# A spectral layer with one table loaded by another queue, two DMAs swapped, and its last steps in another order

## Chip, core and metric

The kernel runs on one core of a Trainium2 chip. The metric is the device time of one execution in microseconds; the time before is the median of nine runs. A profile is of one execution.

## What is computed

Two kinds of layer alternate twice. A is a filter in the frequency domain over the whole 2048 x 1024 input, B is a dense block with the Mish activation; each follows a layer norm and is added to its input.

```python
def _A_ref(x, w_r, w_i):
    X = rfft2(x.astype(float32), axes=(-2, -1))
    X = X * (w_r + 1j * w_i)
    return irfft2(X, s=(S, D), axes=(-2, -1)).astype(bfloat16)

def _B_ref(x, w1, b1, w2):
    h = einsum("bsd,df->bsf", x, w1) + b1
    act = h * tanh(softplus(h))
    return einsum("bsf,fd->bsd", act, w2)

x = x + _A_ref(_layernorm(x), A_w_r, A_w_i)
x = x + _B_ref(_layernorm(x), B_w1, B_b1, B_w2)
x = x + _A_ref(_layernorm(x), A_w_r, A_w_i)
x = x + _B_ref(_layernorm(x), B_w1, B_b1, B_w2)
```

S is 2048, D is 1024, the inner width of B is 3584; inputs and output are bf16.

## The kernel before

The program order of each engine is written out by hand: a helper adds an instruction to an engine's list and works out which semaphores it has to wait for, from the last writers and readers of each buffer. An engine works through its list strictly in order, so an instruction that waits holds up everything listed behind it. This holds for the issuing queues too: SP (SyncE), ACT (ScalarE) and POOL (GpSimd) issue DMAs one after the other, and a DMA that waits for a semaphore holds up the next. All DMAs are issued at L251, so the tiles tell them apart.

Both transforms are products with tables of sines and cosines. A spectral layer (`layer_A`, L711) goes through these stages:

- `s1` (L620): a first short transform along the tokens, for the whole input, into the buffer Y.
- Then eight groups, 0 to 7, each of two of the sixteen remainders of the token frequency. A group goes through four kinds of step, each in two halves (0 and 1). A step is named by three digits: kind, group, half.
  - **2** (`s2`, L733, matmuls L741): the transform along the model dimension, into Z. Half 0 is copied out of PSUM by ACT (L776), half 1 by ACT for groups 0 to 2 and by DVE from group 3 on (L778). In layer 0 a group's filter is put into its layout beside this step (`filter_bins`, matmuls L1002, copies on DVE L1013 and on ACT L1017), beside half 1 for groups 0 and 1 and half 0 for the others.
  - **3** (`s3`, L780, matmuls L786 to L789): the transform along the rest of the tokens with the group's **forward table** (FT). ACT copies the result out (L793), and DVE multiplies it by the filter in four operations (L797, L799, L802, L804), into YK.
  - **4** (`i1`, L807, L815): the inverse of 3 with the group's backward table (BT), copied by ACT (L826) into V; for group 7 half by DVE, half by ACT (L578, L574).
  - **5** (`i2`, L828, L840 and L872): the inverse along the model dimension with the matrix BD, into U: the group's components. ACT copies (L884), DVE for halves 531 and 551 (L882), both for group 7.
- `u_turn` (L886): when half 1 of kind 5 is copied out, the group's components are stored to DRAM (`u_scratch`), and one that was stored before is read back in another layout (`u_back`, L908) into UT. For groups 0 to 6 both are issued by SP: first the store of group g, then the read-back of g - 1. Group 7 is stored by ACT in two halves, and its read-backs are the last ones (`u_last`, L914), by SP and ACT.
- After a few matmuls that keep PE busy (L652, L657), the last short transform (`i4`, L1035, matmuls L1041) reads UT and so waits for all the read-backs. It belongs to the dense layer's start.

Every step takes one of four pairs of PSUM banks in turn, so a step also waits until the step four before it has been copied out; in layer 0 a filter step takes a pair too.

The forward tables sit in a ring of three buffers, as the backward ones do. `open_tables` (L664) loads the first ones: tables 0 and 1, in layer 1 also forward table 2. In layer 0 SP issues these, in layer 1 POOL. The later ones are loaded by POOL in the loop over the steps: the forward table of group g + 2 after step 3, half 1 of group g (L952 to L954). In layer 0 so is forward table 2, after step 301. POOL has other loads in layer 0: the filter rows of groups 2 to 7 (`load_wr`, L984), each as a real and an imaginary part, and the store of the finished filter for layer 1 (`keep_filter`, L1020). SP's list in layer 0 goes on after the tables with small constants, BD among them.

The order of the steps, the same in both layers, is a list of numbers (`order_A`, L976): PE, ACT and DVE all get their instructions in it.

Of the kernel before, what the change touches and what calls it, by code (L numbers as in the profile page):

```python
# [180 lines left out]
class KB:  # L181
# [482 lines left out]
    def open_tables(self, li):  # L664

        self.li = li
        self.WT = self.ring("WT", 4 if li else 8, 2048, [2, 512])
        self.FTr = self.ring("FT", 3, 1536, [2, 384])
        self.BTr = self.ring("BT", 3, 1536, [2, 384])
        if li == 0:  # L670
            self.WR = self.ring("WR", 3, 4096, [2, 2, 512])
        for g in range(2):
            self.load_w(g)
        for g in range(2 + li):
            self.load_tabs(g, li == 0)
        for g in range(2):
            self.load_btabs(g, li == 0)

    def rest_of_filter(self):

        self.WT += [self.alloc(f"WT{i}", self.o["WT"] + 2048 * i, [2, 512]) for i in range(4, 8)]
        gate = Res("gate")
        for r in self.r_xr[1:3]:
            gate.inherit(r)
        for g in (2, 3):
            self.load_w(g, [gate])

    def load_tabs(self, g, sp=False):
        b = self.FTr[g % 3]
        self.dma(self.sp if sp else self.pool, b.ap, self.con["FT"][g], f"ft{g % 3}{sp}", writes=[b.res])  # L690

    def load_btabs(self, g, sp=False):
        b = self.BTr[g % 3]
        self.dma(self.sp if sp else self.pool, b.ap, self.con["BT"][g], f"bt{g % 3}{sp}", writes=[b.res])
# [9 lines left out]
    def load_w(self, g, after=()):  # L704
        if self.li == 0:
            self.load_wr(self.wr(g), g)
            return
        i = 2 * g % 8
        self.dma(self.pool, self.wt_pair(i), self.w_d[g], f"wt{g % 4}", reads=[self.r_wd[g]] + list(after), writes=[w.res for w in self.WT[i:i + 2]])

    def layer_A(self, li):  # L711
# [13 lines left out]
        def filter_bins(g):  # L725
            ps, banks, _ = self.pair()
            self.filter_bins(g, ps, banks, self.wr(g), WT[2 * g % 8:2 * g % 8 + 2], o["WT"] + 2048 * (2 * g % 8),
                             self.JT, self.r_jt, dve)
# [51 lines left out]
        def s3(g, i):  # L780

            ps, banks, _ = self.pair()
            z, ft = zslot(g, i), FT[g % 3]
            t = ft.ap[:, i, :]
            fns = [
                lambda e: e.matmul(ps[:, 0:512], t[:, 0:128], z.ap[:, 0, :], start=True, stop=False),  # L786
                lambda e: e.matmul(ps[:, 512:1024], t[:, 0:128], z.ap[:, 1, :], start=True, stop=False),
                lambda e: e.matmul(ps[:, 512:1024], t[:, 128:256], z.ap[:, 0, :], start=False, stop=True),
                lambda e: e.matmul(ps[:, 0:512], t[:, 256:384], z.ap[:, 1, :], start=False, stop=True),  # L789
            ]  # L790
            self.group(fns, reads=[z.res, ft.res], writes=banks)
            x = X[(2 * g + i) % 4]
            self.op(act, lambda e: e.activation(x.ap.rearrange("p a b -> p (a b)"), ps, ACT.Copy, scale=SIG),  # L793
                    reads=banks, writes=[x.res])
            wt, yk = WT[(2 * g + i) % 8], YK[(2 * g + i) % 6]
            ta, tb = T[2 * i], T[2 * i + 1]
            self.op(dve, lambda e: e.tensor_tensor(ta.ap, x.ap, wt.ap[:, 0:1, :].to_broadcast([P, 2, 512]), ALU.mult),  # L797
                    reads=[x.res, wt.res], writes=[ta.res])
            self.op(dve, lambda e: e.tensor_tensor(tb.ap, x.ap, wt.ap[:, 1:2, :].to_broadcast([P, 2, 512]), ALU.mult),  # L799
                    reads=[x.res, wt.res], writes=[tb.res])  # L800
            yk.res.begin()
            self.op(dve, lambda e: e.tensor_tensor(yk.ap[:, 0, :], ta.ap[:, 0, :], tb.ap[:, 1, :], ALU.subtract),  # L802
                    reads=[ta.res, tb.res], parts=[yk.res])
            self.op(dve, lambda e: e.tensor_tensor(yk.ap[:, 1, :], tb.ap[:, 0, :], ta.ap[:, 1, :], ALU.add),  # L804
                    reads=[ta.res, tb.res], parts=[yk.res])

        def i1(g, i):  # L807

            ps, banks, _ = self.pair()
            yk, bt, v = YK[(2 * g + i) % 6], BT[g % 3], V[g % 2]  # L810
            t = bt.ap[:, i, :]
            fns = []
            for c in range(4):
                for part in range(2):
                    fns.append(lambda e, c=c, part=part: e.matmul(  # L815
                        ps[:, c * 256:(c + 1) * 256], yk.ap[:, part, c * P:(c + 1) * P], t[:, (128, 0)[part]:(384, 256)[part]],
                        start=(part == 0), stop=(part == 1)))
            self.group(fns, reads=[yk.res, bt.res], writes=banks)
            if i == 0:
                v.res.begin()  # L820
            src = ps.rearrange("p (c n) -> p c n", n=P)
            if g == 7:
                for b, prog in enumerate((dve, act)):
                    self.copy(prog, v.ap[:, 4 * b:4 * b + 4, i, :], src[:, 4 * b:4 * b + 4, :], [banks[b]], [], parts=[v.res])
                return
            self.op(act, lambda e: e.activation(v.ap[:, :, i, :], src, ACT.Copy), reads=banks, parts=[v.res])  # L826
# [59 lines left out]
        def u_turn(g, half):  # L886

            u = U[g % 3]
            if g == 7:
                h = slice(8 * half, 8 * half + 8)  # L890
                if half == 0:
                    u_back(6)
                self.dma(act, self.u_d[g][:, h, :], u.ap[:, h, :], f"uwh{half}", reads=[u.res], writes=[self.r_ud7[half]])
                if half:
                    u_last()
            elif half:
                self.dma(sp, self.u_d[g], u.ap, f"uw{g % 3}", reads=[u.res], writes=[self.r_ud[g]])
                if g:
                    u_back(g - 1)

        def open_ut():
# [6 lines left out]
        def u_back(g):  # L908
            if self.UT is None:
                open_ut()  # L910
            self.dma(sp, self.UT.ap[g:P:8, :, :], self.u_d[g].rearrange("l r n -> r l n"), f"usp{g % 3}",
                     reads=[self.r_ud[g]], parts=self.r_ut)

        def u_last():  # L914

            def back(prog, half, q, n):
                l = slice(32 * q, 32 * q + 32 * n)
                self.dma(prog, self.UT.ap[7 + 64 * half:P if half else 64:8, l, :], self.u_d[7][l, 8 * half:8 * half + 8, :].rearrange("l r n -> r l n"),
                         f"ul{half}{q}", reads=[self.r_ud7[half]], parts=self.r_ut[q:q + n])
            back(sp, 0, 0, 2)  # L920
            back(sp, 0, 2, 2)
            for q in range(4):
                back((act, sp)[q % 2], 1, q, 1)
# [17 lines left out]
        for stage, g, h in self.order_A():  # L941
            if stage == 2:
                s2(g, h)
                if li == 0 and h == (g < 2):
                    filter_bins(g)
                    if g in (0, 1):
                        load_w(g + 5)
                    elif g == 4:
                        load_w(7)
            elif stage == 3:  # L950
                s3(g, h)
                if h:  # L952
                    if li <= g < 6:
                        load_tabs(g + 2)  # L954
                    if li == 0:
                        self.keep_filter(g)
                    elif g < 4:
                        load_w(g + 4)
            elif stage == 4:
                i1(g, h)  # L960
                if h and g < 6:
                    load_btabs(g + 2)
            else:
                i2(g, h)
                u_turn(g, h)
# [9 lines left out]
    @staticmethod  # L975
    def order_A():  # L976


        order = ("200 201 210 300 211 301 220 310 400 221 311 401 230 320 410 500 231 321 411 501 330 331 420 510 240 511 421 241 "
                 "250 251 340 341 520 350 430 260 521 431 440 261 351 441 530 531 360 361 450 451 540 541 550 270 551 271 460 461 "  # L980
                 "370 371 560 561 470 471 570 571")
        return [tuple(map(int, w)) for w in order.split()]

    def load_wr(self, wr, g):  # L984
# [798 lines left out]
```

## Time and profile before

| what | value |
|---|---|
| median of 9 runs | 931.34 us (930.1 to 934.52) |
| profiled execution | 934.52 us |
| its span in the profile | 932.7 us |
| PE (matmul) busy | 881.4 us, 94% of the span |
| DVE, ACT, POOL busy | 66%, 47%, 17% |
| first layer A, steps of kinds 2 to 5 | from 37.2 us to the last store at 106.99 us |
| second layer A, the same | from 496.97 us to the last store at 558.33 us |
| share of PE in the chain that ended last | 83% |
| share of DMAs in that chain | 6% |

How to read it: the span is measured inside the core, from the first to the last instruction; the execution's time is a little longer. A row of the timeline gives start, length, engine, line of the kernel, operation and tiles; in brackets is how long the engine stood idle ahead of it, and what ended that idle time. PEld is the load of a matmul's stationary operand and runs beside PE. The chain that ended last is followed back from the last instruction, at each step to what released it. The granted clock is PE's, as a share of full speed.

### The profile page before, as it was taken

What the parts mean: (1) busy time and instruction counts of PE and PEld (TensorE: products, weight loads), DVE (VectorE), ACT (ScalarE), POOL (GpSimd) and SP (SyncE); (2) the same over time, 40 slices, a digit from 0 to 9 for tenths busy, and PEclk for the clock granted to TensorE, in tenths of its full rate; (3) what the DMA queues carried; (4) which work ended last, traced back from release to release, by engine and by line L of the source; (5) the groups of instructions that cost most, each with busy time, mean ns of one, the idle gap of its engine ahead of it and who ended that gap; (6) DMA issues with size and microseconds to landing.
All of it is one profiled execution on the core that took longest, in us unless ns stands there. A gap on an engine that the chain in (4) does not pass through costs nothing.

```text
span 932.7 us, 13616 instructions
## 1 busy us (share of the span) xinstructions
PE 881.4 (94%) x5503; PEld 471.8 (51%) x5503; DVE 619.7 (66%) x985; ACT 436.0 (47%) x645; POOL 159.9 (17%) x187
## 2 busy tenths in 40 slices
PE   0889889999999999999999988999999999999998
PEld 0667476444444444444446766764444444444443
DVE  7788367687689667558866765666747665554473
ACT  7989385456213385520019965847650015552000
POOL 5633003970003652010121200000000000000000
PEclk9999999999999999999999998999999999999999
DMA  9969861684877488364732894444156545732432
GB/s 290 284 203 292 211 182 52 236 283 102 294 243 231 151 306 314 130 211 153 271 108 98 233 220 133 159 154 163 58 189 192 176 150 194 277 119 82 172 123 109
DMA packets 145839, 175.99 MB, mean 189 GB/s; under 512 B 66904, under 2 KB 124344, under 8 KB 145656
## 3 DMA queue, kind: packets, MB, share of 16 engines
q1 hardware_dynamic: 132816, 128.29, 44.4%
q0 software_dynamic: 10864, 45.19, 13.5%
q10 hardware_dynamic: 2096, 1.64, 0.6%
q8 instruction: 43, 0.70, 0.3%
q14 instruction: 20, 0.16, 0.1%
HBM read 130.78 MB, written 40.89 MB: 184 GB/s over the span
## 4 chain that ended last, share of the span: by engine, by line
PE 83%; DMA 6%; DVE 4%; ACT 3%; SPq 2%; POOL 1%; issue 1%; ACTq 0%; DVEq 0%; POOLq 0%
PE PS L1329 33%; PE PS L1230 29%; PE PS L1190 6%; PE PS L815 3%; PE PS L741 3%; DMA ARENA<-in_B_w_dram 2%; PE PS L840 2%; SPq L251 2%; PE PS L1041 2%; POOL ARENA L1123 1%; DMA ARENA<-in_A_x_dram 1%; PE PS L1151 1%; DMA ARENA<-u_scratch 1%; DMA u_scratch<-ARENA 1%; PE PS L786 1%
## 5 line engine op out<-in xcount | busy, mean ns | idle before, releaser
L1329 PE MATMUL PS<-ARENA 128*128 128x512 bf16 x1568 | 340.4, 379 | 0.7 <-DMA ARENA<-in_B_w_dram 0.7
L1230 PE MATMUL PS<-ARENA 128*128 128x512 bf16 (+1 forms) x1288 | 280.5, 379 | 0.8 <-DVE ARENA L1235 0.8
L1329 PEld LDWEIGHTS PS<-ARENA 128*128 128x128 bf16 x1568 | 153.2, 98 | 185.6 <-DVE ARENA L1372 1.0
L1235 DVE TENSOR_TENSOR ARENA<-PS,ARENA 128x512 f32<-128x512 f32 x230 | 157.1, 691 | 101.1 <-PE PS L1230 93.2
L1230 PEld LDWEIGHTS PS<-ARENA 128*128 128x128 bf16 x1288 | 125.3, 98 | 153.5 <-DVE ARENA L1235 3.5
L1240 ACT ACTIVATE ARENA<-ARENA,B 128x512 bf16<-128x512 f32 x138 | 98.8, 721 | 69.3 <-DVE ARENA L1235 64.0
L574 ACT ACTIVATE ARENA<-PS 128x512 f32<-128x512 f32 (+3 forms) x86 | 61.6, 727 | 114.4 <-PE PS L1230 93.1
L1123 POOL TENSOR_TENSOR ARENA<-ARENA 128x512 bf16<-128x512 bf16 x56 | 71.8, 1282 | 74.5 <-DVE ARENA L523 60.4
L452 ACT ACTIVATE ARENA<-XS 128x1024 bf16<-128x1024 bf16 x60 | 63.2, 1053 | 36.3 <-DVE XS L1380 33.0
L1190 PE MATMUL PS<-ARENA 128*128 128x256 bf16 (+1 forms) x528 | 75.1, 300 | 3.2 <-DVE ARENA L1156 1.7
L1354 DVE TENSOR_TENSOR ARENA<-ARENA 128x3584 bf16<-128x3584 bf16 x32 | 63.9, 2017 | 0.0
L1190 PEld LDWEIGHTS PS<-ARENA 128*128 128x128 bf16 x528 | 51.0, 99 | 23.0 <-DVE ARENA L1156 3.2
L1380 DVE TENSOR_TENSOR XS<-PS,ARENA 128x512 bf16<-128x512 f32 x52 | 35.8, 690 | 39.3 <-PE PS L1329 39.0
L1372 DVE TENSOR_TENSOR ARENA<-PS,ARENA 128x512 f32<-128x512 f32 x48 | 32.9, 687 | 27.4 <-PE PS L1329 27.0
L1194 ACT ACTIVATE ARENA<-PS,B 128x256 bf16<-128x256 f32 (+1 forms) x66 | 33.2, 516 | 31.0 <-PE PS L1190 30.8
L1240 ACT ACTIVATE ARENA<-PS,B 128x512 bf16<-128x512 f32 x46 | 31.5, 685 | 18.3 <-PE PS L1230 18.3
L1368 DVE TENSOR_TENSOR ARENA<-ARENA,XS 128x512 f32<-128x512 f32 x52 | 36.8, 731 | 0.6
L797 DVE TENSOR_TENSOR ARENA<-ARENA 128x1024 bf16<-128x1024 bf16 x32 | 22.0, 689 | 22.3 <-ACT ARENA L793 16.6
L443 ACT ACTIVATE RS<-MV,EPS 128x1 f32<-128x1 f32 (+2 forms) x11 | 3.3, 296 | 71.6 <-DVE MV L565 70.1
L793 ACT ACTIVATE ARENA<-PS 128x1024 bf16<-128x1024 f32 x32 | 32.7, 1050 | 7.4 <-PE PS L789 7.4
L815 PE MATMUL PS<-ARENA 128*128 128x256 bf16 x256 | 32.9, 276 | 3.3 <-DVE ARENA L804 3.2
L741 PE MATMUL PS<-FD,ARENA 128*128 128x256 bf16 (+1 forms) x256 | 31.8, 271 | 2.5 <-ACT ARENA L641 1.3
(100 smaller groups left out, 824.5 us busy)
## 6 DMA issues: line engine op xcount, KB each, us to landing
ARENA<-in_B_w_dram SPq DMA_DIRECT2D x30, 896.0 KB, 6.7
ARENA<-w1s_scratch SPq DMA_DIRECT2D x28, 896.0 KB, 4.6
ARENA<-w2s_scratch SPq DMA_DIRECT2D x24, 896.0 KB, 6.2
w1s_scratch<-ARENA POOLq DMA_DIRECT2D x14, 896.0 KB, 4.4
ARENA<-in_B_w_dram SPq DMA_DIRECT2D x24, 512.0 KB, 4.5
u_scratch<-ARENA SPq DMA_DIRECT2D x14, 512.0 KB, 3.5
ARENA<-u_scratch SPq DMA_DIRECT2D x14, 512.0 KB, 5.9
w2s_scratch<-ARENA POOLq DMA_DIRECT2D x8, 896.0 KB, 4.2
```

The source lines that it names most:

```text
L452: self.op(act, lambda e, i=i, f=f: e.activation(junk.ap, x, f, accum_out=sums[:, i:i + 1]), reads=[self.r_xs[j]], writes=[junk.res], parts ...
L574: fn = (lambda e: e.activation(dst, src, ACT.Copy)) if scale is None else \
L741: fns.append(lambda e: e.matmul(dst, at(r), FD[:, t:t + n], start=start, stop=stop))
L815: fns.append(lambda e, c=c, part=part: e.matmul(ps[:, c * 256:(c + 1) * 256], yk.ap[:, part, c * P:(c + 1) * P], t[:, (128, 0)[part]:(384, ...
L1123: self.op(self.pool, lambda e, dst=A(dst), x=A(x), y=A(y), op=op: e.tensor_tensor(dst, x, y, op), reads=[b.res] + list(after), writes=[b.rs])
L1190: fns.append(lambda e, db=db, bank=bank, fl=fl: e.matmul(PS[:, bank, 0:w], wb.ap[:, db, fl * P:(fl + 1) * P], x.ap[:, db, tok], start=(db ...
L1230: self.group([lambda e, db=db: e.matmul(PS[:, bank, :], A[:, db, :], mov[:, db, :], start=(start and db == 0), stop=(db == 3), skip_group_ ...
L1235: self.op(dve, lambda e: e.tensor_tensor(dst.ap, PS[:, bank, :], x.ap, ALU.add), reads=[self.r_bank[bank], x.res], writes=[dst.res])
L1240: self.op(act, lambda e: e.activation(at, src, ACT.Mish, bias=self.B1[:, ft:ft + 1]), reads=[res, self.r_b1], writes=[ra])
L1329: self.group([lambda e, i=i, k=k, b=PB[n][k].ap: e.matmul(PS[:, bank, :], ap[:, i, t * P:(t + 1) * P], b[:, i - 7 * k, :], start=(start an ...
L1354: self.op(dve, lambda e: e.tensor_tensor(ap[dst][:, f, :], ap[x][:, f, :], ap[y][:, f, :], op), reads=part(x, k) + part(y, k), writes=part ...
L1368: self.op(dve, lambda e: e.tensor_tensor(a[t], a[t], x, ALU.add), reads=[rx], writes=[r[t]])
```

## The change

There are three parts.

1. In `open_tables` the loop loads forward tables 0 and 1 in both layers, and table 2 after the two backward tables. So layer 0 issues table 2 on SP in `open_tables`, and no longer on POOL after step 301; in layer 1 it stays on POOL and goes behind the two backward tables.
2. In `u_turn` group 6 reads back group 5 first and then stores itself, both still on SP. The other groups are as before.
3. In `order_A` steps 270 and 271 (with group 7's filter step in layer 0) stand earlier, ahead of 450 and ahead of 540; 551 follows 550; 370 stands ahead of 461. On ACT and DVE the copies and products move with their steps. POOL's store of group 7's filter follows 371 as before. The list behind 461 371 is as it was.

```diff
-        for g in range(2 + li):
+        for g in range(2):
             self.load_tabs(g, li == 0)
         for g in range(2):
             self.load_btabs(g, li == 0)
+        self.load_tabs(2, li == 0)
...
             elif half:
+                if g == 6:
+                    u_back(5)
                 self.dma(sp, self.u_d[g], u.ap, f"uw{g % 3}", reads=[u.res], writes=[self.r_ud[g]])
-                if g:
+                if 0 < g < 6:
                     u_back(g - 1)
...
                 if h:
-                    if li <= g < 6:
+                    if 1 <= g < 6:
                         load_tabs(g + 2)
...
         order = ("200 201 210 300 211 301 220 310 400 221 311 401 230 320 410 500 231 321 411 501 330 331 420 510 240 511 421 241 "
-                 "250 251 340 341 520 350 430 260 521 431 440 261 351 441 530 531 360 361 450 451 540 541 550 270 551 271 460 461 "
-                 "370 371 560 561 470 471 570 571")
+                 "250 251 340 341 520 350 430 260 521 431 440 261 351 441 530 531 360 361 270 450 451 271 540 541 550 551 460 370 "
+                 "461 371 560 561 470 471 570 571")
```

## The prediction

> **What bounds the kernel now.** I read the page's busy shares first: PE is busy 94% of the span, and the chain that ended last is 83% PE. So only a stretch in which PE stands still, or runs at a lower clock, can give time back. Then I read the waits, longest first, kept those whose waiter is PE, and looked at both spectral stages (first layer 37 to 115 us, second 497 to 565 us), which are all that the change touches. The largest such wait on a DMA in the first layer is this one, and the chain in order of time passes through it:
>
> ```profile
> PE PS L786 <- DMA ARENA<-c_ft: 3.4, 1, 3.4
> ```
> ```profile
> 46.61 1.44 POOL ARENA L251 x2
> 48.05 5.96 DMA ARENA<-c_ft
> 56.02 1.41 PE PS L815 x8
> ```
>
> The third forward table is the third DMA in POOL's line behind group 6's two filter loads, which themselves wait until 46.61. It lands at 54.0. The timeline shows what waited, and who waited for that:
>
> ```profile
> 53.52 1.36 DVE L1013 COPY ARENA<-ARENA 128x1024 bf16<-128x1024 bf16 x2
> 54.15 0.59 PE L786 MATMUL PS<-ARENA 128*128 128x512 bf16 x1 [3.42 <-DMA ARENA<-c_ft]
> 56.05 1.02 ACT L793 ACTIVATE ARENA<-PS 128x1024 bf16<-128x1024 f32 x1 [2.69 <-PE PS L789]
> 57.11 0.69 DVE L797 TENSOR_TENSOR ARENA<-ARENA 128x1024 bf16<-128x1024 bf16 x1 [2.23 <-ACT ARENA L793]
> ```
>
> PE is idle for 3.42 us ahead of step 320, then ACT for 2.69, then DVE for 2.23. The table by windows shows the after-effect (columns: window, length, busy time of PE, PEld, DVE, ACT, POOL, then granted clock):
>
> ```profile
> 54.00:57.20 3.20, 3.05 (x12) 1.65 (x13) 0.97 (x3) 1.02 (x1) 0.00 (x0) 0.53 1.03 400
> ```
>
> The clock is halved after that gap. From 60 to 84 us the same table has PE busy 24.0 of 24.0 us, so a time won at 60 is kept until step 360.
>
> The other place is the end of the stage. Second layer:
>
> ```profile
> 549.52 0.69 DVE L797 TENSOR_TENSOR ARENA<-ARENA 128x1024 bf16<-128x1024 bf16 x1 [2.38 <-ACT ARENA L793]
> 551.67 1.05 PE L815 MATMUL PS<-ARENA 128*128 128x256 bf16 x8 [0.61 <-DVE ARENA L804]
> 553.67 1.05 PE L815 MATMUL PS<-ARENA 128*128 128x256 bf16 x8 [0.95 <-DVE ARENA L804]
> 555.50 1.48 PE L840 MATMUL PS<-ARENA,BD 128*128 128x256 bf16 x12 [0.79 <-DVE ARENA L578]
> 557.27 0.33 ACTq L251 DMA_DIRECT2D u_scratch<-ARENA  x1
> ```
>
> PE has run out of other work, and the last group's products on DVE (two sets of four operations) decide when steps 470 and 471 start, and so when the last components are stored (557.27) and the next stage begins. SP's line:
>
> ```profile
> 552.27 0.32 SPq L251 DMA_DIRECT2D u_scratch<-ARENA  x1
> 552.63 11.24 SPq L251 DMA_DIRECT2D ARENA<-u_scratch  x6
> ```
>
> **Part 1, the third table.** Layer 0 only; in layer 1 it trades places with two other loads on POOL at 400 us, over 100 us ahead of its use (508.7), worth nothing. It is now issued by SP after the fourth table, at about 37.2. The loads beside it took 5.3 to 7.5 us to land, so it is there by 45, needed at 50.8. Step by step without the wait:
> - PE is free at 50.73, and so is the bank of 320 (ACT's copy of 311 ends at 50.76). 320 takes 0.87: 51.7. ACT, busy until 53.36, copies it at once and is done at 54.4.
> - DVE is busy without a gap until 54.88 (the copies of L1013, first line above), so 320's four products start at 54.88 instead of 57.11. They take 2.09 (57.11 to 59.20), then 231's copy 1.23: 58.20.
> - Step 330 reads what that copy wrote: PE at 58.25 instead of 61.60. **Gain 3.35.**
>
> PE alone would allow more: the seven steps 320 to 501 took 10.87 us, of which 3.42 is the wait and 1.38 the low clock (320 and 410 took 1.66 and 1.45 instead of 0.86 and 0.87), so 61.60 - 4.80 = 56.80, a gain of 4.80. What is late next is DVE, and 1.45 of PE's gain becomes waiting there. After 330, ACT and DVE are early by as much or more (330's products at 60.35 against 63.87), and what stands behind the old load on POOL (the fourth table among it) is issued about 1.4 us earlier, so 3.35 is kept.
>
> What the load is moved past: on SP the small constants behind it go 0.5 us later. Of them the backward matrix BD is the first needed, by step 500: issued 37.67, 11.0 us to land, 48.7; with half a microsecond of issue and 0.6 of bytes, 49.8, against a step now due at 52.6. [...] The windows from 36 to 44 us moved 317 to 341 GB/s, so 192 KB more take an estimated 0.6 us from others in flight. The tightest is group 2's imaginary filter: issued 37.10, 6.6 to land, 43.7, used by PE at 44.20. [...] I take 0: ACT, not PE, paces 41 to 53.
>
> **Part 2, group 5 read back ahead of group 6's store.** The same two SP instructions (0.54 and 0.32 us) in the other order. The gain, a read-back that is off the engines about 1 us sooner, meets the last store's landing (3.7 and 3.2 us; 3.6 and 4.3 in layer 0): between 0 and 0.4 a layer. The cost: the read-back waits for store 5, and store 6 and its own read-back are queued behind it on SP. Store 5 would go at 546.96 (below), lands 3.1 to 5.3 us later as stores 4 and 5 did, 550.1 to 552.3, plus 0.54: 552.8 at worst, against store 6 ready at 552.75. Cover is thin but real; without it each microsecond delays only store 6's read-back, which has until about 560. I take 0, with -0.4 to +0.3 for the range.
>
> **Part 3, the order.** Work on PE is the same; 270 and 271 move ahead of 540, 551 ahead of 460, 370 ahead of 461. Each step takes 0.87 on PE, 541 and 551 1.08. Layer 1, 360 at 536.39: ahead of 370 now stand nine steps of 0.87 and two of 1.08, so 370 is at 546.38 instead of 547.31. Its copy starts 0.20 after the step and takes 1.02; DVE starts 0.05 later, 548.52. The first products end at 550.62, before PE reaches 470 (about 551.5): that wait of 0.61 goes. The second set starts 2.01 after the first, 550.53 (371's copy is done at 550.42), ends 552.63; 471 at 552.68 instead of 553.67. **Gain 1.0**; DVE's second set still is last. New waits: 560 needs 461's copy, which stands behind 370's on ACT, 549.49 against PE free at 548.99: 0.5 us, paid out of the time in which PE would have waited for 470. Store 5 goes at 551's copy, 544.43 + 1.28 + 1.22 = 546.96 (before 546.04).
>
> Layer 0 has group 7's filter step too, moved with 270: four matmuls (0.46 on PE), two ACT copies (0.88), two DVE copies (1.40), and POOL's store of it, which nothing waits for and which leaves the busy tail of the stage (it was issued at 94.36). Counted from 360: DVE does 360's and 361's products until 6.2, the filter copies until 7.5, 271's copy until 8.75. 551 needs that bank; PE is there at 8.50, waits 0.3. 370 at 10.75, 471 at 17.04 instead of 17.80 (102.33 - 84.53). **Gain 0.75**, bounded by 0 (a copy later than I have it) and 1.0.
>
> **Sum.** 3.35 + 0.75 + 1.0 = 5.1. The profiled execution took 934.52 (span 932.7 and 1.8 around it): 929.4. The median of the runs shown is 931.34, 3.2 lower, and I move the sum to it: **926.2**. After the stages the chain is PE and DMAs issued when PE frees a buffer, so it shifts as a whole.
>
> **Rivals.**
> - *The tail gives nothing* (0.17): the last store and the last read-backs (3.7 + 4.3 us on the chain) now overlap more with group 6's read-back, which goes 0.4 later while they go 1.0 earlier; each loses what part 3 won. Part 1 alone: 928.0. For it: 256-byte-row read-backs took 4.9 to 6.7 us, when two overlap longest. Against: the last stores are half as large.
> - *PE's own gain* (0.13): DVE and ACT follow closer than I have them, 4.8 in part 1, plus 0.4 a layer of part 2: 923.9.
> - *The move does not do what it says* (0.06): the table still lands late, or another load (BD, the next table on POOL) holds PE at the same place, and the tail gives nothing or 1 us: 930.5 to 931.3.
> - *Slower* (0.04): the wait on SP. If store 5 lands later than about 9 us after issue, store 6's read-back is issued after the last store has landed, at 560, and the next stage waits for it: from there each microsecond counts in both layers. At 15 us, 2 x 6 - 5.1 = 7 us slower, 938. Stores took 3.1 to 5.5, so it is far from deciding.
> - The forecast itself: 0.60, 925 to 927.5.
>
> **Chances.** 0.2% is 1.9 us, about what a measurement of this kernel can tell from no change. Faster by more: the forecast, PE's own gain and the tail that gives nothing, 0.90, less a little for a mixture of small misses: 0.88. Within: 0.08. Slower: 0.04. Range 923.7 to 928.6: it takes in PE's own gain and the bare part 1 with part 2's 0.3 a layer.
>
> **What would show it.** Step 320 follows 311's copy with no wait for c_ft; the clock stays near 1.00 between 54 and 57; PE waits about 1 us before 330, for DVE. 360 starts near 81.2. 470 has no wait, 471 still waits for L804, about 1 us earlier counted from 360; 560 waits for ACT. It is wrong if another DMA stops PE between 44 and 60, if store 6 goes late on SP, or if the last store's landing grows.

## The result, and the profile after

The changed kernel takes 927.68 us (median of 18 runs, 925.96 to 929.47) beside 931.76 for the kernel before: a ratio of 0.9956, 95% interval 0.9946 to 0.9966, a gain of 4.1 us (3.2 to 5.0). In a second comparison it took 928.8 beside 931.7: 0.9973 (0.9961 to 0.9984), a gain of 2.5 by that ratio. The two together say about 3.3; 5.1 were forecast. The profiled execution took 928.0, its span is 926.2.

In the changed kernel the lines stand one to three further down: L741 is L742, L786 is L787, L793 is L794, L815 is L816, L1041 is L1044. In the experiments below they move by one or a few more.

The third table first. This is the timeline of the changed kernel around steps 320 and 330; the rows are ACT's copy of 311, PE for 320, DVE's filter copies, the first of 320's products, DVE's copy of 231, and PE for 330:

```profile
50.47 1.16 ACT L794 ACTIVATE ARENA<-PS 128x1024 bf16<-128x1024 f32 x1
51.68 0.39 PE L787 MATMUL PS<-ARENA 128*128 128x512 bf16 x1
...
54.40 1.38 DVE L1016 COPY ARENA<-ARENA 128x1024 bf16<-128x1024 bf16 x2
55.69 0.68 DVE L798 TENSOR_TENSOR ARENA<-ARENA 128x1024 bf16<-128x1024 bf16 x1
...
57.69 1.22 DVE L779 CAST ARENA<-PS 128x1024 bf16<-128x1024 f32 x1
...
58.97 0.39 PE L787 MATMUL PS<-ARENA 128*128 128x512 bf16 x1 [0.96 <-DVE ARENA L779]
```

Step 320 (51.68) follows 311's copy and has no wait for the table any more. The filter copies of L1016, 320's products right behind them, the copy of 231 (L779), and then PE for step 330 after 0.96 us of waiting: the chain that the prediction named as late next. The windows of the same execution, and below them the first of these windows in before:

```profile
37.00:41.00 4.00, 3.96 (x24) 2.99 (x25) 1.37 (x2) 2.12 (x3) 4.00 (x5) 0.57 1.08 397
54.00:57.20 3.20, 3.20 (x28) 2.29 (x26) 3.17 (x7) 3.20 (x5) 0.60 (x2) 1.00 1.02 378
60.00:84.00 24.00, 24.00 (x225) 18.15 (x223) 21.55 (x37) 22.09 (x28) 7.44 (x11) 1.00 0.73 224
```
```profile
37.00:41.00 4.00, 3.75 (x32) 2.88 (x33) 1.44 (x2) 2.83 (x6) 4.00 (x7) 1.00 1.07 357
```

The clock at 54 is 1.00 (it was 0.53), as foreseen. At 37 it is 0.57, where it was 1.00 before; the last section comes back to this.

The end of the second layer, PE's rows and ACT's last store of group 7:

```profile
545.74 1.48 PE L841 MATMUL PS<-ARENA,BD 128*128 128x256 bf16 x12 [0.35 <-ACT ARENA L827]
...
547.71 1.05 PE L816 MATMUL PS<-ARENA 128*128 128x256 bf16 x8
548.95 1.05 PE L816 MATMUL PS<-ARENA 128*128 128x256 bf16 x8 [0.19 <-DVE ARENA L805]
...
561.22 0.95 PE L1044 MATMUL PS<-MT,ARENA 128*128 128x32 bf16 x32 [0.77 <-DMA ARENA<-u_scratch]
```
```profile
553.60 0.33 ACTq L251 DMA_DIRECT2D u_scratch<-ARENA  x1
```

The rows are steps 560, 470 and 471 and the start of the last transform. Step 560 waits 0.35 for ACT, 470 not at all, 471 0.19 for DVE. Counted from step 360 (532.59), 471 starts at 16.36 instead of 17.28 and the last store at 21.01 instead of 21.94: part 3's 0.9 us is there. But the last transform (L1044) starts at 28.63, where it started at 28.62. The gain turned into a wait, the last bracket. In before, PE waited for these read-backs 0.51 us in the first layer and 0.16 in the second (there within the transform, not ahead of its first matmul). The lists of waits, for both layers together, before and then changed:

```profile
PE PS L815 <- DVE ARENA L804: 3.2, 4, 1.0
...
PE PS L1041 <- DMA ARENA<-u_scratch: 0.7, 2, 0.5
```
```profile
PE PS L1044 <- DMA ARENA<-u_scratch: 2.0, 2, 1.2
...
PE PS L787 <- DVE ARENA L779: 1.0, 1, 1.0
...
PE PS L816 <- DVE ARENA L805: 0.4, 2, 0.2
```

The wait of L816 for the products fell from 3.2 to 0.4 us, that of L1044 for the read-backs rose from 0.7 to 2.0. Last, SP's line in the second layer:

```profile
543.11 2.63 SPq L251 DMA_DIRECT2D u_scratch<-ARENA  x1
545.78 3.75 SPq L251 DMA_DIRECT2D ARENA<-u_scratch  x2
549.58 1.52 SPq L251 DMA_DIRECT2D u_scratch<-ARENA  x1
554.92 5.34 SPq L251 DMA_DIRECT2D ARENA<-u_scratch  x5
```

These are store 5, the read-backs of 4 and 5, store 6, and the last read-backs, group 6's the first of them; a row of several DMAs takes in the time between them. Store 5 took 2.63 us to issue and landed 5.9 after its start, the read-back of 5 waited for it, and store 6, ready at 548.85, went at 549.58. Group 6's read-back went at 554.92, only 0.6 us ahead of the first one of group 7; in before it was 5.5 us ahead (555.43 against 560.96).

### The profile page after: what moved, and what is told of

It is laid out like the page before. It is cut to its first block, busy times and chain, and to the rows that moved or that the text cites. A ratio compares the mean times of both kernels' runs of the same rounds, so it can differ in the third digit from the quotient of the medians.

```text
span 926.2 us, 13613 instructions
## 1 busy us (share of the span) xinstructions
PE 879.1 (95%) x5503; PEld 470.1 (51%) x5503; DVE 619.9 (67%) x985; ACT 436.6 (47%) x645; POOL 158.7 (17%) x186
## 4 chain that ended last, share of the span: by engine, by line
PE 85%; DVE 5%; DMA 4%; ACT 3%; SPq 2%; issue 1%; ACTq 0%; DVEq 0%
PE PS L1332 36%; PE PS L1233 30%; PE PS L1193 6%; PE PS L742 3%; PE PS L816 2%; PE PS L841 2%; SPq L251 2%; PE PS L1044 2%; DMA ARENA<-in_A_x_dram 1%; DMA ARENA<-u_scratch 1%; PE PS L1154 1%; DMA u_scratch<-ARENA 1%; ACT ARENA L452 1%; PE PS L652 1%; ACT ARENA L641 1%; PE PS L873 1%
## 5 line engine op out<-in xcount | busy, mean ns | idle before, releaser
L742 PE MATMUL PS<-FD,ARENA 128*128 128x256 bf16 (+1 forms) x256 | 33.0, 278 | 2.5 <-ACT ARENA L641 1.3
L794 ACT ACTIVATE ARENA<-PS 128x1024 bf16<-128x1024 f32 x32 | 33.1, 1054 | 4.3 <-PE PS L790 4.3
L816 PE MATMUL PS<-ARENA 128*128 128x256 bf16 x256 | 32.6, 273 | 0.4 <-DVE ARENA L805 0.4
```

Of the source, the lines that this page charges most:

```text
L742: fns.append(lambda e: e.matmul(dst, at(r), FD[:, t:t + n], start=start, stop=stop))
L816: fns.append(lambda e, c=c, part=part: e.matmul(ps[:, c * 256:(c + 1) * 256], yk.ap[:, part, c * P:(c + 1) * P], t[:, (128, 0)[part]:(384, ...
```

## The experiments

Below, "from 360" is the time from step 360 to the first matmul of the last transform, and "wait" is PE's wait for the read-backs ahead of it (for before in the second layer: within it), first layer / second layer. "From 360" and "wait" are read from one execution each.

**The parts one by one.** Part 1 alone; parts 1 and 3; part 2 alone; part 3 alone. Each is the kernel before with these hunks of the change:

```diff
 e1, e2
-        for g in range(2 + li):
+        for g in range(2):
...
+        self.load_tabs(2, li == 0)
...
-                    if li <= g < 6:
+                    if 1 <= g < 6:
 e3
+                if g == 6:
+                    u_back(5)
...
-                if g:
+                if 0 < g < 6:
 e2, e4
-"... 360 361 450 451 540 541 550 270 551 271 460 461 370 371 560 561 470 471 570 571"
+"... 360 361 270 450 451 271 540 541 550 551 460 370 461 371 560 561 470 471 570 571"
```

> The third forward table loaded by SP, and nothing else. Theory A (part 1 is worth what was forecast, the rest was eaten by the swap of the read-back): 330 about 3.3 us earlier counted from the first matmuls of step 200, if the clock there is full; the time from 360 to the first matmul of the last short transform as before, 30.9 us in layer 0 and 28.6 in layer 1; total 3.3 us below before. Rival B (part 1 gives PE's whole 4.8, and the tail costs): total 4.5 or more below before, less than the changed kernel's time. On the low clock at 37 to 41 us that the profile of the changed kernel shows: if the earlier load causes it, this profile shows it too; if it is chance, either.

> Parts 1 and 3 without the swap: group 6 is stored ahead of group 5's read-back. Theory A (the swap holds store 6 on SP until store 5 has landed and lets it share the engines with a read-back): store 6 lands in about 3.1 us again, group 6's read-back is issued some 3 us earlier counted from 360, and the time from 360 to the first matmul of the last short transform is 30.1 in layer 0 and 27.7 in layer 1, each 0.8 to 1.0 below before; total 1 to 1.8 us below the changed kernel. Rival C (the DMA engines need a fixed time for the last stores and read-backs, whatever their order): 30.8 and 28.6, total as the changed kernel.

> Group 5's read-back ahead of group 6's store, in the old order of steps and with the old table load. Theory A: store 5 goes at 546.0 and lands 5.3 us later, so the read-back is issued at 551.4, just ahead of store 6; store 6 lands in about 5.3 instead of 3.1 us, and the time from 360 to the first matmul of the last short transform grows by 0 to 1 us a layer; total 0 to 2 us above before. Rival C: no change, total as before. A swap that helps (the reason for which it could have been made) would shorten it by up to 0.4 a layer.

> Another order of the steps alone, with the old table load and the old SP order. Theory A: 470 and 471 at 17.0 us from 360 in layer 0 and 16.4 in layer 1 for the second of them, as in the changed kernel, and this gain arrives at the last short transform: 30.1 and 27.7 from 360; total 1.7 us below before. Rival C: the second of them the same, but 30.8 and 28.6 at the transform; total within 0.3 us of before.

| kernel | ratio to before (95% interval) | median us | from 360 | wait |
|---|---|---|---|---|
| before | | 931.03 | 30.89 / 28.62 | 0.51 / 0.16 |
| part 1 (e1) | 0.9972 (0.9957 to 0.9988) | 929.76 | 31.04 / 29.33 | 0.65 / 0.55 |
| parts 1, 3 (e2) | 0.9977 (0.9964 to 0.9991) | 929.24 | 30.80 / 29.90 | 1.22 / 2.04 |
| part 2 (e3) | 1.001 (0.9987 to 1.0033) | 932.39 | 31.72 / 30.04 | 1.33 / 1.26 |
| part 3 (e4) | 0.9995 (0.9978 to 1.0011) | 931.41 | 31.08 / 29.15 | 1.49 / 1.28 |

Part 1 is worth 2.6 us (1.1 to 4.0). Parts 2 and 3 alone are worth nothing that can be measured. In every kernel with part 3 step 471 comes 0.80 and 0.92 us earlier, and in both such kernels of this table the wait for the read-backs grows by 0.7 to 1.9. Theory A, which had the lost gain in the swap of part 2 and expected 30.1 / 27.7 without it, falls: e2 and e4 have no swap, and their last transforms start 0.7 to 2.2 us later than that.

e3 and e4 still load the third table on POOL, and so show what part 1 removes, in two more executions. Step 320 in e4 and then in e3:

```profile
52.34 0.38 PE L786 MATMUL PS<-ARENA 128*128 128x512 bf16 x1 [2.03 <-DMA ARENA<-c_ft]
```
```profile
53.70 0.38 PE L786 MATMUL PS<-ARENA 128*128 128x512 bf16 x1 [1.73 <-ACT ARENA L776]
```

The wait, 3.42 in the profile of before, is 2.03 here and 1.73 there (in e3 the table landed at 53.5, about as late as the copy named). The load took 6.0, 4.6 and 4.4 us. So the execution from which part 1 was priced had the longest of three waits.

**Is the swap worth something in the new order?** The changed kernel and the one without part 2, side by side.

> The changed kernel once more, beside the same kernel without the swap of part 2 (next run), to tell what the swap is worth in the new order. In the separate sessions so far the changed kernel stood at a ratio of 0.9956 and the one without the swap at 0.9977, a difference of 2.0 us with an uncertainty of about 1.6. Theory S (the swap matters once the order is new: in the profiles the last transform of the second layer started 28.6 us after step 360 with it and 29.9 without): the changed kernel is 1.3 to 2 us below the other one again. Theory N (chance: the landing of the last read-backs scatters by about 0.7 us, and the clock near 37 us comes and goes by 1.4 us): the two are within 0.8 us. The ratio against before stays near 0.996 (0.9946 to 0.9966) by both.

> Parts 1 and 3 without part 2, once more, in the session of the changed kernel. Theory S: ratio near 0.9975, 1.3 to 2 us above the changed kernel. Theory N: ratio near 0.9965, within 0.8 us of it.

Ratios 0.9973 (0.9961 to 0.9984) and 0.9971 (0.9959 to 0.9983), medians 928.8 and 929.17: 0.4 us between the medians, as theory N (chance) had it. From 360: 31.02 / 28.26 with the swap, 30.96 / 28.97 without. A smaller effect is not excluded. In the second layer the four traces with the swap in the new order (the changed kernel, e5, and e11 and e12 below) start the last transform at 28.63, 28.26, 28.02 and 27.86, the three without it (e2, e6, e4) at 29.90, 28.97 and 29.15: about 1 us apart. The first layer shows no such difference (30.6 to 31.1 in all seven), and by the times the swap is worth 2.0 us in the first comparison and -0.2 in this one. The profile of e5 has no low clock at 37 (1.00) and shows part 1 cleanly: ACT's copy of 330 starts 21.97 after the first step of the stage, against 25.60 in before.

**Group 6's read-back taken out of the tail.** From the changed kernel; `u_back` gets the source group as a second argument, and group 6's rows are read early from group 0's components. So this kernel leaves out the read-back of group 6's own components, and serves only to measure:

```diff
                 if half == 0:
-                    u_back(6)
...
                 if 0 < g < 6:
                     u_back(g - 1)
+                if g == 1:
+                    u_back(6, 0)
```

> The changed kernel with group 6's read-back taken out of the tail: the rows of group 6 are filled early from group 0's components, beside group 0's own read-back, so a part of the values differs from the reference. Group 6 is still stored. This tells apart where part 3's 0.8 us (first layer) and 0.92 us (second layer) went, by which the last store is earlier and the last transform is not. Theory D (the last stores and their read-backs share the DMA engines with group 6's read-back, and closing up makes them overlap more): group 7's second half store lands in 2.2 to 3.2 us in both layers (now 4.4 and 2.5), the last transform starts 6.3 to 7 us after that store's issue (now 9.1 and 7.6), and the kernel is 2 to 3.5 us faster than the changed kernel, 924 to 926 us. Theory E (fixed latency and the slow issue of the last read-backs on the SP queue set the end): 7.4 us or more after the store in both layers, and the time within 1 us of the changed kernel.

Ratio 0.9937 (0.9919 to 0.9956), median 926.2, 2.6 us below the changed kernel of the same comparison. From 360: 29.43 / 27.87, and no wait in either layer. The last transform is now held by PE's own matmuls, not by DMAs. So it is group 6's read-back, at this place, that holds the last transform up, as theory D said. One number of theory D missed: in the first layer the last store still landed in 3.9 us, and the transform came 7.8 after it. And the run does not tell apart two ways in which that read-back could hold up the others: by its bytes (the sharing of theory D), or by its place on SP ahead of the last read-backs (the slow issue of theory E).

**Group 6 by halves**, to win that with nothing left out (`u_back6` reads the two halves back, one DMA each):

```diff
-                    u_back(6)
+                    u_back6()
...
+            elif g == 6:
+                h = slice(8 * half, 8 * half + 8)
+                if half:
+                    u_back(5)
+                self.dma(sp, self.u_d[g][:, h, :], u.ap[:, h, :], f"uw6{half}", reads=[u.res], writes=[self.r_ud6[half]])
             elif half:
-                if g == 6:
-                    u_back(5)
...
```

> The changed kernel with group 6 stored and read back by halves: half 0 is stored as soon as step 560 is copied out, as group 7's halves are; the order on the SP queue is store of half 0, group 5's read-back, store of half 1, then both read-backs of group 6. Same bytes, two more DMAs on SP. Theory D (sharing of the engines): the first half leaves the engines about 0.9 us sooner, so the last transform starts 0.2 to 0.6 us earlier in each layer, time 0.4 to 1.2 us below the changed kernel. Theory E (issue on SP sets the end): two more issues of 0.5 to 1 us each ahead of the last read-backs, 0.5 to 1.5 us later in each layer, time 1 to 3 us above the changed kernel.

0.998 (0.9967 to 0.9992), median 929.72: 0.9 us above the changed kernel, within the uncertainty. From 360: 31.49 / 28.79, 0.5 later than the changed kernel of this comparison in both layers. Theory D had forecast 0.2 to 0.6 earlier, theory E 0.5 to 1.5 later. So nothing is won by cutting the transfer, and this run speaks for issue on SP as a part of the cause.

**Is part 3 worth its 1.7 us without that read-back?** The kernel of e7 with the old order, and e7 again:

```diff
-"... 360 361 270 450 451 271 540 541 550 551 460 370 461 371 560 561 470 471 570 571"
+"... 360 361 450 451 540 541 550 270 551 271 460 461 370 371 560 561 470 471 570 571"
```

> As the run with group 6's read-back taken out of the tail (its rows are filled early from group 0's components, so a part of the values differs from the reference), but with the order of steps of before: parts 1 and 2 without part 3. Beside the next run it asks what part 3 is worth once that read-back is out of the way. Theory D (part 3's gain was eaten by the overlap of the last stores with group 6's read-back): now the gain comes through, so this kernel is 0.8 + 0.92, about 1.7 us slower than the next (1.2 to 2.2), and its last transform starts about 0.8 and 0.9 us later counted from step 360. Theory F (the last stores and read-backs end at a time set by all the bytes of the stage's last groups, group 5's and 6's stores too, whatever the order): the two are within 0.7 us, and the last transform starts at the same distance from step 360.

> The same kernel as in the earlier run with group 6's read-back out of the tail (a part of the values differs from the reference), new order, as the partner of the run before it. Ratio near 0.9937 again; by theory D 1.2 to 2.2 us faster than with the old order, by theory F within 0.7 us.

927.67 and 925.79, ratios 0.9947 (0.9926 to 0.9967) and 0.9924 (0.9901 to 0.9948): 1.9 us between the medians. The intervals overlap; the traces decide. PE at the end of the second layer, old order, then new:

```profile
530.57 0.39 PE L787 MATMUL PS<-ARENA 128*128 128x512 bf16 x1
...
559.18 0.95 PE L1045 MATMUL PS<-MT,ARENA 128*128 128x32 bf16 x32
```
```profile
532.65 0.39 PE L787 MATMUL PS<-ARENA 128*128 128x512 bf16 x1
...
560.35 0.95 PE L1045 MATMUL PS<-MT,ARENA 128*128 128x32 bf16 x32
```

The first row is step 360, the last the start of the last transform, and no bracket follows it: 559.18 - 530.57 = 28.61 and 560.35 - 532.65 = 27.70, 0.91 apart. In the first layer it is 30.25 and 29.42, 0.83 apart. With the read-back out of the way part 3 gives what the prediction had worked out (0.75 and 1.0), to a tenth. Theory F (the order can't matter) falls, and that group 6's read-back is what ate the gain stands.

**Is DVE what is late next after the table?** Group 3's filter copies, just ahead of 320's products, moved to POOL; and, since that failed, kept on DVE but issued ahead of 330's products.

```diff
 e11
-                             self.JT, self.r_jt, dve)
+                             self.JT, self.r_jt, pool if g == 3 else dve)
 e12
-            self.op(eng, lambda e, dst=dst, src=src: e.tensor_copy(dst, src), reads=[wr.res], parts=parts)
+            copy = lambda dst=dst, src=src: self.op(eng, lambda e: e.tensor_copy(dst, src), reads=[wr.res], parts=parts)
+            self.late.append(copy) if g == 3 else copy()
...
+                if (li, g, h) == (0, 3, 0):
+                    for copy in self.late:
+                        copy()
                 s3(g, h)
```

> The changed kernel with group 3's two filter copies (1.39 us on DVE, just ahead of step 320's products) on POOL. It tests the step of the prediction that says that DVE is what is late next after the third table: PE waits 0.96 us before step 330 for DVE's copy of step 231, behind 320's products, behind these copies. By that theory 320's products start when ACT's copy of 320 is done, about 0.5 us earlier, 330 starts 0.4 to 0.6 us earlier counted from the first step, and PE's wait falls to 0.4 to 0.6; time 0 to 0.6 us below the changed kernel. If instead PE's own work or ACT set step 330, it doesn't move. It could also become slower, by 1 us or more, if POOL's slower copies hold up the loads queued behind them or the filter is late for step 330's products.

932.88 us, ratio 0.9997 (0.998 to 1.0014), 2 to 4 us above the changed kernel's two ratios: a miss, and no answer. ACT's copy of 330 comes 27.27 after the stage's first step instead of 21.97. Its timeline:

```profile
50.05 5.09 DVE L1016 COPY ARENA<-ARENA 128x1024 bf16<-128x1024 bf16 x2
...
52.88 2.76 POOL L1016 COPY ARENA<-ARENA 128x1024 bf16<-128x1024 bf16 x2
...
57.65 1.89 PE L816 MATMUL PS<-ARENA 128*128 128x256 bf16 x8 [3.97 <-DVE ARENA L805]
```

DVE's copies for group 2, 1.39 us elsewhere, took 5.09, ending half a microsecond before POOL's, and PE waited 3.97 us for DVE.

> The changed kernel with group 3's two filter copies (1.39 us on DVE) kept on DVE but issued later: not ahead of step 320's products but just ahead of step 330's, which are the first to read them. It asks again what the run with these copies on POOL could not, since there POOL's copies and DVE's ran at the same time and DVE's pair took 5.09 us in place of 1.39: is DVE what is late next behind the third table? If it is, 320's products start as soon as ACT's copy of 320 is done, about 0.5 us earlier, and with them the copy of 231 and step 330: PE's wait ahead of 330 falls from 0.96 to about 0.5, and 330 is 0.4 to 0.5 earlier counted from the first step. Because DVE still has the same work, its products for 330 cannot be earlier, so step 360 gains less, 0 to 0.4, and the time is within 0.5 us of the changed kernel. If PE or ACT sets 330, neither 330 nor 360 moves, or 360 is later by as much as 330's products are pushed back.

```profile
55.65 0.69 DVE L799 TENSOR_TENSOR ARENA<-ARENA 128x1024 bf16<-128x1024 bf16 x1 [0.70 <-ACT ARENA L795]
...
58.93 0.39 PE L788 MATMUL PS<-ARENA 128*128 128x512 bf16 x1 [0.45 <-DVE ARENA L780]
```

DVE now waits for ACT's copy of 320, and PE's wait ahead of 330 is 0.45 instead of 0.96. ACT's copy of 330 starts 21.46 after the first step instead of 21.97 and that of 360 at 44.40 instead of 44.90: half a microsecond, kept. So DVE was late next. The time, 927.67, ratio 0.9974 (0.9956 to 0.9992), cannot be told from the changed kernel's; of the versions that leave nothing out it is the best by its trace, not measurably by its time.

## Why the prediction was right, and where its sum was not

The forecast was 926.2 in a range of 923.7 to 928.6; 927.68 and 928.8 were measured, the second just above the range. The direction and the main cause are right. About 1.8 us of the 5.1 are missing, and the measured time lies on the rival "the tail gives nothing" (928.0). The range holds 927.68 because it reached up to part 1 alone, not because the three gains arrived. The runs bear that rival out in the first layer; in the second the four executions with the swap keep between none and 0.8 of part 3's 0.9 us.

- **Part 1, the chain.** Confirmed step by step, and with it the rival "PE's own gain" falls: no wait at 320, clock 1.00, 0.96 us before 330 for DVE (about 1 foreseen). From the stage's first step, 330 starts at 20.89 in e1 and 24.40 in before: 3.51, against 3.35. Step 360 keeps all 3.51. e12 confirms that DVE set it. Moving BD and the filter loads cost nothing that shows: no run shows the 0.6 us that the table was to take from the loads beside it. In the changed kernel BD took 9.9 us to land (11.0 in before) and group 2's imaginary filter 5.8 (6.6), and PE waits for no DMA between 37 and 84 us.
- **Part 1, its size.** 3.35 was read from one execution. By the same count (24.40, e4 23.30, e3 22.53, against 20.89, or 21.93 for the changed kernel, which like e3 had the low clock at 37) the gain is 3.5, 2.4 and 0.6. Timed, it is 2.6 (1.1 to 4.0). And the sum was moved to the median as it stood: the profiled execution was 3.2 us above its median. Since its wait was the longest of the three, part of that excess was probably the very wait that the change takes out, which could not be won from the median a second time; three executions can't prove it.
- **Part 2.** Taken at 0; measured as nothing clear of the noise (1.001 alone, 0.9987 to 1.0033; 0.4 us between medians in the new order). Two details were wrong on the way. Store 5 landed 5.9 us after issue, beyond the 3.1 to 5.3 allowed, so store 6 was held 0.7. Store 6 then landed in 5.3 us instead of 3.1, and group 6's read-back went 22.33 us after step 360, against 19.04 in before: 3.3 later, where the prediction had 0.4. And alone (e3) the swap does lengthen the wait for the read-backs, by 0.8 and 1.1 us; in the new order it doesn't (1.43 and 0.39 in e5, 1.36 and 1.10 in e6), and in the second layer it seems to help, as said above. Why was not tried.
- **Part 3, the steps.** 471 at 17.00 and 16.36 from 360, foreseen 17.04 and 16.29: gains of 0.80 and 0.92 for 0.75 and 1.0. The waits of 560 (0.35) and 471 (0.19) are as named, and 470's is gone.
- **Part 3, its worth: the step that failed.** "After the stages the chain is PE and DMAs issued when PE frees a buffer, so it shifts as a whole." It does not. The last read-backs were level with PE already (waits of 0.51 and 0.16), so when PE came 0.80 and 0.92 earlier it waited: 1.19 and 0.77 us in the changed kernel, 1.43 and 0.39 in e5. e9 and e10 show it from the other side: without group 6's read-back the gain is there. How that read-back holds up the last ones differs. Without the swap the transfers took longer: in e2's second layer group 6's read-back and the last half store took 7.1 and 5.3 us, against 4.9 and 3.2 in before.

```profile
ARENA<-u_scratch SPq DMA_DIRECT2D x1, 512.0 KB, 7.1
```
```profile
u_scratch<-ARENA ACTq DMA_DIRECT2D x1, 256.0 KB, 5.3
```

With the swap the store doesn't take longer, but the issue on SP does. This is the chain that ended last, second layer, in before and then in the changed kernel: group 7's first half store, two read-backs issued by SP, and the landing of a third.

```profile
557.27 3.67 DMA u_scratch<-ARENA
560.96 0.61 SPq L251
...
561.61 0.59 SPq L251
...
562.25 4.28 DMA ARENA<-u_scratch
```
```profile
552.54 2.99 DMA u_scratch<-ARENA
...
555.55 1.40 SPq L251
...
557.00 0.89 SPq L251
...
557.93 4.75 DMA ARENA<-u_scratch
```

The store landed in 2.99 us instead of 3.67, but the two issues took 2.29 us instead of 1.20, and the landing 0.5 longer. The profile of before had the sign: 0.7 us of PE waiting for u_scratch in the list of waits, a small row that the prediction passed over.

What stays open: how much of the lost gain goes to shared bytes and how much to issue on SP; what the swap is worth in the second layer; and whether the 4.1 and the 2.5 us of the two comparisons differ by more than chance. Within a kernel the last transform's start moved by 0.4 us (28.63 and 28.26 in the second layer of the changed one) and the low clock near 37 by more.

## What to carry to other kernels

Before a gain is carried past a stage, look at what the next stage waits for: a small wait for a DMA (here 0.51 and 0.16 us) can mean that the DMA is level with the engine, and then, as here, an earlier engine wins little unless the transfers end earlier too. If the profiled execution lies above the median, ask whether the wait that the change removes is part of that excess; two or three profiles of kernels that share the wait (here 3.4, 2.0 and 1.7 us) price it better than one. To find what ate a gain, take the suspect away in both versions and see whether the gain comes back; this names the culprit, but not yet the way in which it acts.

## What the runs showed of the hardware

- Issuing a DMA on SP was not of fixed length. In the second layer of before SP's stores took 0.32 to 0.35 us each, 2.6 us or more behind the read-back ahead of them. In the changed kernel stores 5 and 6, 1.8 and 0.6 us behind a read-back, took 2.63 and 1.52 (2.28 and 1.42 in e5). That the read-back was still in flight was not enough to slow a store: in before the store of 546.04 took 0.32 us while the read-back of 543.46, which took 5.3 to land, was under way. What sets the length was not tried.
- DVE's copies beside POOL's took much longer in e11: 5.09 us for a pair that takes 1.39. DVE's pair began at 50.05, 2.8 us ahead of POOL's copies (52.88), and ended at 55.14, half a microsecond before POOL's (55.64). What held DVE is not shown.
- The clock between 37 and 41 us was 0.57 to 0.72 in six of the fourteen profiles (the changed kernel's first, e2, e3, e6, e8 and e10) and 1.00 in the others, before's and the changed kernel's second included. The gap ahead of step 200 was 1.16 us with the low clock (the changed kernel, e3) as with the full one (before, e1, e4, e5, e12). The low clock puts step 310 1.4 us later (8.88 us after step 200 in the changed kernel, 7.46 in before), and 1.0 of that was still there at step 330 in the first profile. What makes the clock low here is not shown.
- Behind PE's gap ahead of step 320 the clock from 54 to 57.2 us was 0.53 after 3.42 us (before), 0.54 after 2.03 (e4) and 1.00 after 1.73 (e3). The low clock cost time: from step 320 to step 321 e4 took 5.15 us, e3 3.48.
